# Two engines on one score group: the exponential on ScalarE and VectorE's first read of the third bank, with no order declared between them

## The chip, the cores and the metric

The kernel runs on one core of one Trainium2 chip. The metric is the device time of one execution in microseconds (us). Before the change it is 943.0 us, the median of 3 runs (941.9 to 944.33). The profile is that of one further execution, whose span is 944.2 us. The chip's engines run side by side, each through its own list of instructions in a fixed order, and they meet only through waits: TensorE multiplies matrices into PSUM, ScalarE and VectorE read PSUM and write SBUF.

## What is computed

The reference is a stack of four layers on a sequence of 2048 tokens of 448 features: softmax attention with 16 heads, then a dense block with a squared ReLU, and both once more. Each adds to `x`.

```python
def _A_ref(x, wqkv, wo):                      # attention, 16 heads of 28
    qkv = (x @ wqkv) ...                      # q, k, v: [1, 16, 2048, 28]
    scores = jnp.einsum("bhqd,bhkd->bhqk", q, k) * Dh ** -0.5
    p = _softmax(scores, axis=-1)
    o = jnp.einsum("bhqk,bhkd->bhqd", p, v)
    return o... @ wo
def _B_ref(x, w1, b1, w2, b2):                # dense, relu(h) ** 2
    h = jnp.einsum("bsd,df->bsf", x, w1) + b1
    r = jnp.where(h > 0, h, 0)
    return jnp.einsum("bsf,fd->bsd", r * r, w2) + b2

x = x + _A_ref(_layernorm(x), A_wqkv, A_wo)
x = x + _B_ref(_layernorm(x), B_w1, B_b1, B_w2, B_b2)
x = x + _A_ref(_layernorm(x), A_wqkv, A_wo)
x = x + _B_ref(_layernorm(x), B_w1, B_b1, B_w2, B_b2)
```

One layer of attention has 16 x 2048 x 2048 = 67 million scores, and each needs one exponential. The two layers of attention are where nearly all of the time lies.

## The kernel before

The scores come in **units**: one head, 256 queries, two blocks of 128 keys, which is 128 partitions x 512 columns in float32, one PSUM bank. A **group** is one tile `sc` of three banks, and there are two such tiles in turn (`ps_sc`, `bufs=2`). TensorE fills a group (line 781), ScalarE takes the exponential of it in one instruction (line 799) into `pt`, and TensorE later multiplies `pt` by the values (line 940). Two further single banks, named `mt`, serve all other products.

ScalarE would have to take all of the exponentials. So the kernel gives some units to VectorE, which computes 2^x from integer and polynomial steps. Its first operation on such a unit, the **take** (line 853), is the only one that reads the scores from PSUM; the other five work on SBUF. There are two places from which a unit is taken:

- a fourth unit of the group in one of the `mt` banks (`own` is true). ScalarE then does three banks and VectorE a bank of another tile;
- the third bank of the group's own tile (`own` is false). ScalarE then does two banks, 1024 columns, of that tile, and VectorE reads the third bank of the same tile. Only this kind is concerned by the change.

```python
def s_stream():                                  # TensorE: fills the groups
    ...
        sc = ps_sc.tile([P, 3 * 512], DT.float32, name="sc", tag="sc")
        dst = [sc[:, k * 512:k * 512 + 512] for k in range(len(us))]
        ...
            if not own:                          # the third bank goes to VectorE
                us, ks = us[:2], ks[:2]
                gbuf[gi]["n"] = 2
            us, ks = us + [units[j]], ks + [3]
            if own:
                ...                              # a bank of its own: dst.append(bank(x, "mt"))
            else:
                x = gbuf[gi]["x"] = o            # the same tile: freed by two readers
                o.need = 2
            pl.spawn(C_PRIO, a_unit(gi, x, dst[-1], us[-1], passes[us[0][0]][0]))
        ...
            nc.tensor.matmul(dst[k][...], lhsT=K_sb..., rhs=Q_sb..., start=True, stop=True, ...)   # L781

def e_stream():                                  # ScalarE: the exponentials
    ...
        pt = gbuf[gi]["pt"] = ptp.tile([P, 3 * 512], DT.bfloat16, name="pt")
        nc.scalar.activation(out=pt[:, 0:n], in_=gbuf[gi]["sc"][:, 0:n], func=AF.Exp,       # L799
                             scale=float(np.log(2.0)) * 2.0 ** -FRAC)
    o = gbuf[gi]["e"] = Op("ACT", n / 1200 + 0.05, fn, deps=[("s", gi)], acq=R_pt, need=n // 512,
                           rel=gbuf[gi]["s"], sets=("e", gi))

def a_unit(gi, x, src, unit, l):                 # VectorE: one unit
    ...
        nc.vector.tensor_scalar(out=box["i"], in0=two(src), scalar1=EXP_BIAS,               # L853
                                scalar2=EXP_LOW, op0=ALU.add, op1=ALU.max)
    c = Op("DVE", 0.69, take, deps=[("s", gi)], acq=sets_of(unit), rel=x)
    yield c
    pl.spawn(..., a_rest(...))                   # L863, L868 (three times), L874: in SBUF
```

The order of the instructions on each engine is fixed when the kernel is built: a planner (`Planner`) keeps a model of the clock of each engine, asks when an operation's `deps` have ended, and issues the earliest. In this model the exponential and the take of a group each depend on the group's matmuls, `("s", gi)`, and not on one another. The waits that end up in the program are drawn by the framework from the tiles that the instructions touch: two instructions of different engines on one tile of PSUM are put in the order in which they were issued, even when both only read.

Of the kernel before, what the change touches and what calls it, by code (L numbers as in the profile page):

```python
# [12 lines left out]
AF = mybir.ActivationFunctionType  # L13
ALU = mybir.AluOpType
# [11 lines left out]
FRAC = 16  # L26
EXP_BIAS = -0.207249953 * 2.0 ** FRAC
EXP_LOW = -56.0 * 2.0 ** FRAC
# [180 lines left out]
def kernel(  # L209
# [12 lines left out]
    nc = tc.nc  # L222
# [438 lines left out]
    gbuf = []  # L661
# [7 lines left out]
    def sets_of(unit):  # L669

        pi, kb, r, hh = unit
        l, qb, *_ = passes[pi]
        if l == 0:
            return R_v if 2 <= qb <= 6 else R_v[:1]
        return R_v
# [41 lines left out]
    def s_stream():  # L717
# [69 lines left out]
            yield o  # L787
        s_left.clear()

    def e_stream():  # L790
        gi = 0
        while gi < len(gbuf) or s_left:
            yield Op("-", 0.0, None, deps=[("s", gi)])
            n = gbuf[gi]["n"] * 512

            def fn(e, gi=gi, n=n):
                e_now[:] = [e_now[0] + n // 512 + ("x" in gbuf[gi]), gi]
                pt = gbuf[gi]["pt"] = ptp.tile([P, 3 * 512], DT.bfloat16, name="pt")
                nc.scalar.activation(out=pt[:, 0:n], in_=gbuf[gi]["sc"][:, 0:n], func=AF.Exp,  # L799
                                     scale=float(np.log(2.0)) * 2.0 ** -FRAC)  # L800
            o = gbuf[gi]["e"] = Op("ACT", n / 1200 + 0.05, fn, deps=[("s", gi)], acq=R_pt, need=n // 512,
                                   rel=gbuf[gi]["s"], sets=("e", gi))
            yield o
            gi += 1
# [25 lines left out]
    def set_of(res, l):  # L830

        k = R_v.index(res)
        two = lambda a: a.rearrange("p (a n) -> p a n", a=2)
        if k == 0:
            i, h = two(v_i[:, :]), two(v_h[:, :])
        else:
            keys = K_sb[1 - l][:, :, S - 512:S] if l == 0 else K_sb[0][:, :, 0:512]
            i, h = keys[:, 0:2, :].bitcast(DT.int32), keys[:, 2:4, :].bitcast(DT.float32)
        return i, h, two(v_e[k][:, :]), two

    def a_unit(gi, x, src, unit, l):
        yield Op("-", 0.0, None, deps=[("s", gi)])
        b0, b1, b2, b3 = [b * 2.0 ** (FRAC * (4 - k)) for k, b in enumerate(EXP_POLY)]
        box = {}

        def take(e):
            pending[0] -= 1
            box["i"], box["h"], box["e"], two = set_of(c.res, l)
            box["two"] = two
            halves = box["i"].bitcast(DT.uint16).rearrange("p a (n t) -> p a n t", t=2)  # L850
            box["f"] = halves[:, :, :, 0]
            box["n"] = box["i"].bitcast(DT.int16).rearrange("p a (n t) -> p a n t", t=2)[:, :, :, 1]
            nc.vector.tensor_scalar(out=box["i"], in0=two(src), scalar1=EXP_BIAS,  # L853
                                    scalar2=EXP_LOW, op0=ALU.add, op1=ALU.max)
        c = Op("DVE", 0.69, take, deps=[("s", gi)], acq=sets_of(unit), rel=x)
        yield c
        pl.spawn(lambda now: V_LATE if now > c.end + V_WAIT else V_PRIO, a_rest(gi, c, box, unit, (b0, b1, b2, b3)))

    def a_rest(gi, c, box, unit, bs):
        b0, b1, b2, b3 = bs  # L860

        def power(e):
            nc.vector.tensor_scalar(out=box["e"], in0=box["n"], scalar1=128.0, scalar2=128.0 * EXP_FIELD,  # L863
                                    op0=ALU.mult, op1=ALU.add)

        def step(b, begin=False):
            def fn(e):
                nc.vector.scalar_tensor_tensor(out=box["h"], in0=box["f"] if begin else box["h"], scalar=b,  # L868
                                               in1=box["f"], op0=ALU.add, op1=ALU.mult)
            return fn  # L870

        def close(e):
            pd = gbuf[gi]["pd"] = pd_of(o)
            nc.vector.scalar_tensor_tensor(out=box["two"](pd), in0=box["h"], scalar=b0,  # L874
                                           in1=box["e"].bitcast(DT.bfloat16), op0=ALU.add, op1=ALU.mult)
        h = Op("DVE", 0.68, step(b3, True), deps=[c])
        yield h
        p = Op("DVE", 0.42, power, deps=[c])
        yield p
        for b in (b2, b1):  # L880
            h = Op("DVE", 0.68, step(b), deps=[h])
            yield h
        o = Op("DVE", 0.68, close, deps=[h, p], acq=lambda: pd_free(unit), rel=c, sets=("x", gi))
        gbuf[gi]["x"] = o
        yield o
# [248 lines left out]
    pl.spawn(9.5, heat())  # L1134
    pl.spawn(0, s_stream())
    pl.spawn(1, e_stream())
    pl.spawn(2, p_stream())
    pl.clock["PE"] = 1.2
# [38 lines left out]
```

The softmax here doesn't subtract the row's maximum and nothing guards it: scores larger than these inputs give would overflow.

## Time and profile before

| | |
|---|---|
| time, median of 3 runs | 943.0 us (941.9 to 944.33) |
| span of the profiled execution | 944.2 us |
| ScalarE busy | 886.2 us (94%) |
| TensorE matmuls busy | 844.7 us (89%) |
| VectorE busy | 782.5 us (83%) |
| exponentials of three banks | 592, mean 1500 ns |
| exponentials of two banks | 76, mean 1047 ns |
| takes from `sc` | 75, some 0.69 us each |
| takes from `mt` | 45, some 0.69 us each |
| granted TensorE clock, mean | 0.989 |

A profile counts an engine as busy while an instruction of its runs. The idle time in front of an instruction is put down to whichever instruction of another engine ended last among those it waited for: "`ACT pt L799` waits for `DVE v_i L853`" says that an exponential stood idle until a take had ended. PE, DVE and ACT are TensorE, VectorE and ScalarE; names as `pt<-sc` give the tile written and the tile read. The exponentials run from 11.1 us to 924.0 us of the span, so what lies ahead of them and after them is 31 us in all.

### The profile page before, as it was taken

Reading aid. Unit: us, or ns where it says so; the run is one execution under the profiler, and the core shown is the slowest. Engines: PE = TensorE matmul, PEld = TensorE weight load, DVE = VectorE, ACT = ScalarE, POOL = GpSimd, SP = SyncE. Lnnn points to the kernel's source line nnn. Section 1 sums busy time; section 2 is a strip of 40 time slices with the busy share of each in tenths; the row PEclk is TensorE's granted clock in tenths of the full one; section 3 lists DMA queues with packets and bytes.
Section 4 is the critical chain, followed back from the end, with each engine's and each line's share of the span. In section 5 each row is a group of like instructions: output and inputs, shape, how many; then the busy total and the mean of one; then the engine's idle time right before and its main releaser. Section 6 shows DMA issues by size and latency. Waiting matters only on the chain.

```text
span 944.2 us, 29595 instructions
## 1 busy us (share of the span) xinstructions
PE 844.7 (89%) x13089; PEld 469.1 (50%) x13089; DVE 782.5 (83%) x1595; ACT 886.2 (94%) x688; POOL 42.9 (5%) x100
## 2 busy tenths in 40 slices
PE   8999888899989889998998999888988889988898
PEld 4555545354454444545444454444444545445465
DVE  7755889988999889979888888898898888888864
ACT  6999999998999999999999899999999999999993
POOL 4100000000000000010000000000000000000000
PEclk9999999999999999999999899999999999999999
DMA  7100010000000000000000000011000000000000
GB/s 233 52 2 2 9 38 14 14 13 9 13 14 9 14 14 8 14 14 2 2 2 2 1 2 1 2 43 32 23 14 18 13 23 8 24 13 19 25 9 21
DMA packets 32989, 18.47 MB, mean 20 GB/s; under 512 B 17498, under 2 KB 32411, under 8 KB 32860
## 3 DMA queue, kind: packets, MB, share of 16 engines
q1 hardware_dynamic: 32860, 16.58, 6.0%
q8 instruction: 102, 1.67, 0.7%
q14 instruction: 27, 0.22, 0.1%
HBM read 14.26 MB, written 2.07 MB: 17 GB/s over the span
## 4 chain that ended last, share of the span: by engine, by line
ACT 46%; PE 21%; DVE 18%; issue 13%; POOL 1%; DMA 1%; POOLq 0%; ACTq 0%; SPq 0%
ACT pt L799 46%; PE mt L532 9%; PE sc L781 7%; PE oT L940 3%; DVE v_h L868 2%; DVE K_sb L868 2%; DVE K_sb L853 2%; DVE v_i L853 2%; DVE r L1077 1%; DVE v_e L863 1%; DVE st L425 1%; PE mt L1128 1%; DVE xn L498 1%; DVE V_sb L874 1%; DVE x_sb L1034 1%
## 5 line engine op out<-in xcount | busy, mean ns | idle before, releaser
L799 ACT ACTIVATE pt<-sc 128x1536 bf16<-128x1536 f32 (+1 forms) x668 | 875.5, 1449 | 33.7 <-PE sc L781 15.9
L781 PE MATMUL sc<-Q_sb,K_sb 32*128 32x256 bf16 (+1 forms) x5966 | 328.1, 266 | 72.1 <-ACT pt L799 52.9
L781 PEld LDWEIGHTS <-K_sb 32*128 32x128 bf16 x6102 | 161.4, 92 | 249.9 <-issue 241.5
L940 PE MATMUL oT<-pt,V_sb 128*32 128x256 bf16 (+1 forms) x4104 | 155.5, 271 | 1.6 <-DVE K_sb L964 0.8
L532 PE MATMUL mt<-xnT,w 128*128 128x256 bf16 (+1 forms) x888 | 119.0, 272 | 6.6 <-DVE r L1077 2.7
L940 PEld LDWEIGHTS <-V_sb 128*32 128x32 bf16 x4352 | 93.8, 96 | 53.9 <-issue 50.3
L868 DVE SCALAR_TENSOR_TENSOR K_sb<-K_sb 128x512 f32<-128x512 uint16 x165 | 112.6, 683 | 0.7 <-PE mt L532 0.2
L532 PEld LDWEIGHTS <-w 128*128 128x128 bf16 x952 | 79.7, 98 | 41.4 <-issue 32.6
L868 DVE SCALAR_TENSOR_TENSOR v_h<-v_h,v_i 128x512 f32<-128x512 f32 x130 | 88.7, 683 | 0.5
L1077 DVE TENSOR_SCALAR r<-mt 128x512 bf16<-128x512 f32 x105 | 71.9, 685 | 16.1 <-PE mt L532 15.9
L532 PE MATMUL mt<-w,V_sb 128*128 128x448 bf16 (+1 forms) x288 | 68.8, 353 | 0.0
L1128 PE MATMUL mt<-xn,ident 128*128 128x448 bf16 x133 | 46.3, 359 | 3.9 <-DVE x_sb L1034 0.9
L447 POOL TENSOR_TENSOR ve<-mv,eps_t 128x2 f32<-128x2 f32 (+1 forms) x34 | 9.6, 282 | 884.1 <-DVE mv L426 814.1
L1034 DVE TENSOR_TENSOR x_sb<-x_sb,mt 128x448 bf16<-128x448 bf16 (+1 forms) x64 | 39.0, 610 | 7.1 <-PE mt L532 6.8
L868 DVE SCALAR_TENSOR_TENSOR v_h<-v_i 128x512 f32<-128x512 uint16 x65 | 44.5, 684 | 0.3
L853 DVE TENSOR_SCALAR K_sb<-sc 128x512 int32<-128x512 f32 x38 | 26.1, 688 | 18.1 <-ACT pt L799 15.1
L425 DVE BATCH_NORM_STATS2 st<-x_sb 128x6 f32<-128x448 bf16 x64 | 39.5, 617 | 1.1 <-DMA x_sb<-in_A_x_dram 0.8
L532 PEld LDWEIGHTS <-V_sb 128*128 128x128 bf16 x302 | 25.6, 98 | 24.9 <-issue 9.5
L853 DVE TENSOR_SCALAR v_i<-sc 128x512 int32<-128x512 f32 x37 | 25.4, 687 | 15.0 <-ACT pt L799 13.6
L498 DVE TENSOR_SCALAR xn<-x_sb,mv,rstd 128x448 bf16<-128x448 bf16 x64 | 25.3, 419 | 12.7 <-POOL rstd L448 12.4
L532 PE MATMUL mt<-xnT,wq 128*128 128x256 bf16 x248 | 35.2, 281 | 0.0
L532 PE MATMUL mt<-xnT,wk 128*128 128x256 bf16 x240 | 33.3, 276 | 0.1
(102 smaller groups left out, 789.8 us busy)
## 6 DMA issues: line engine op xcount, KB each, us to landing
rec<-scr SPq DMA_DIRECT2D x56, 128.0 KB
x_sb<-in_A_x_dram SPq DMA_DIRECT2D x8, 224.0 KB
out_dram<-x_sb SPq DMA_DIRECT2D x15, 112.0 KB
w<-in_B_w_dram SPq DMA_DIRECT2D x1, 1568.0 KB
w<-in_B_w_dram SPq DMA_DIRECT2D x1, 1344.0 KB
dn<-oT_sb SPq DMA_DIRECT2D x56, 4.0 KB
scr<-dn SPq DMA_DIRECT2D x56, 4.0 KB
V_sb<-in_A_wqkv_dram SPq DMA_DIRECT2D x1, 672.0 KB
```

The lines of the kernel that those rows point to most:

```text
L425: nc.vector.bn_stats(out=st[:, :], in_=x_sb[:, t0 + j, :])
L447: nc.gpsimd.tensor_tensor(out=ve[:, a:b], in0=mv[0][:, a:b, 1], in1=eps_t[:, a:b], op=ALU.add)
L498: nc.vector.tensor_scalar(out=xn[:, 0:D], in0=x_sb[:, t0 + j, :], scalar1=mv[0][:, j, 0:1], scalar2=ln[j], op0=ALU.subtract, op1=ALU.mult)
L532: nc.tensor.matmul(box["t"][:, c0:c0 + n], lhsT=lhsT() if callable(lhsT) else lhsT, rhs=rhs, start=a, stop=b)
L781: nc.tensor.matmul(dst[k][:, i * nt * P:(i + 1) * nt * P], lhsT=K_sb[l][rows, g, (kb + i) * P:(kb + i + 1) * P], rhs=Q_sb[rows, g, t0 * P: ...
L799: nc.scalar.activation(out=pt[:, 0:n], in_=gbuf[gi]["sc"][:, 0:n], func=AF.Exp, scale=float(np.log(2.0)) * 2.0 ** -FRAC)
L853: nc.vector.tensor_scalar(out=box["i"], in0=two(src), scalar1=EXP_BIAS, scalar2=EXP_LOW, op0=ALU.add, op1=ALU.max)
L868: nc.vector.scalar_tensor_tensor(out=box["h"], in0=box["f"] if begin else box["h"], scalar=b, in1=box["f"], op0=ALU.add, op1=ALU.mult)
L940: nc.tensor.matmul(box["t"][DHP * hh:DHP * hh + DHP, 0:n], lhsT=V_sb[l][:, kb + i, 4 * g + hh, :], rhs=p[:, c0:c0 + n], start=begin and kb ...
L1034: nc.vector.tensor_tensor(out=x_sb[:, tb, lo:hi], in0=x_sb[:, tb, lo:hi], in1=t[:, 0:hi - lo], op=ALU.add)
L1077: nc.vector.tensor_scalar(out=r[:, 0:w], in0=t[:, 0:w], scalar1=0.0, scalar2=None, op0=ALU.max)
L1128: nc.tensor.matmul(t[:, 0:D], lhsT=ident[:, :], rhs=xns[0][:, 0:D], start=True, stop=True)
```

## The change

For the groups whose third bank goes to VectorE, the exponential and the take are declared to need no order between them. Whichever of the two is issued second drops its wait for the first. Both still wait for the group's matmuls, and the matmuls that fill the tile anew still wait for both. No operation is added, removed, resized or moved in its engine's list. The aim is that two engines which only read, from different banks, do so at the same time.

```diff
+    def apart_from(gi, t):
+
+        if "read" in gbuf[gi]:
+            tc.declare_no_dep(t.ins, gbuf[gi]["read"].ins, reason="both read the scores, in banks of their own")
+        gbuf[gi]["read"] = t
+
     def e_stream():
 ...
-                nc.scalar.activation(out=pt[:, 0:n], in_=gbuf[gi]["sc"][:, 0:n], func=AF.Exp,
-                                     scale=float(np.log(2.0)) * 2.0 ** -FRAC)
+                t = nc.scalar.activation(out=pt[:, 0:n], in_=gbuf[gi]["sc"][:, 0:n], func=AF.Exp,
+                                         scale=float(np.log(2.0)) * 2.0 ** -FRAC)
+                if gbuf[gi].get("x") is gbuf[gi]["s"]:
+                    apart_from(gi, t)
 ...
-            nc.vector.tensor_scalar(out=box["i"], in0=two(src), scalar1=EXP_BIAS,
-                                    scalar2=EXP_LOW, op0=ALU.add, op1=ALU.max)
+            t = nc.vector.tensor_scalar(out=box["i"], in0=two(src), scalar1=EXP_BIAS,
+                                        scalar2=EXP_LOW, op0=ALU.add, op1=ALU.max)
+            if x is gbuf[gi]["s"]:
+                apart_from(gi, t)
```

## The prediction
> **What bounds the kernel now.** I read the page first (busy times, then the chain that ended last), then the groups of ScalarE's instructions with different shapes kept apart, then the waits of the exponential's line and of the take's line, and last the timeline around single groups.
>
> ```profile
> PE 844.7 (89%) x13089; PEld 469.1 (50%) x13089; DVE 782.5 (83%) x1595; ACT 886.2 (94%) x688; POOL 42.9 (5%) x100
> ACT 46%; PE 21%; DVE 18%; issue 13%; POOL 1%; DMA 1%; POOLq 0%; ACTq 0%; SPq 0%
> ```
>
> ScalarE is busiest, and the exponential's line alone is 46% of the chain. But 18% of the chain runs through VectorE and 21% through TensorE: the chain leaves ScalarE again and again. Asked by stretches, ScalarE is busy 861.6 of the 894 us between 30 and 924 us. So it idles 32 us there, and that is all that any change of waits can win in the long stretch. The groups by shape say where:
>
> ```profile
> L799 ACT ACTIVATE pt<-sc 128x1536 bf16<-128x1536 f32 x592 | 808.5, 1500 | 17.3 <-PE sc L781 15.9 <-PE oT L940 0.2
> L799 ACT ACTIVATE pt<-sc 128x1024 bf16<-128x1024 f32 x76 | 78.0, 1047 | 16.4 <-DVE K_sb L853 9.7 <-DVE v_i L853 6.3
> ```
>
> The number after the second bar is the idle time in front of the group, then who ended it. The 76 short exponentials (75 of them share their tile with a take) stand idle 16.4 us, 16.0 of it for the take on their own tile. The 592 long ones idle 17.3 us, nearly all for scores. The take's own line gives the other direction, first what it waited for, then who waited for it:
>
> ```profile
>   ACT pt L799: 28.7, 29
> ...
>   ACT pt L799: 16.0, 27
>   PE sc L781: 15.0, 25
> ```
>
> VectorE stands 28.7 us in 29 takes until the exponential of the same tile ends. And 25 times TensorE waits for a take, 15.0 us, before it can refill the tile. Both kinds stand side by side near 322 us:
>
> ```profile
> 319.75 2.42 ACT L799 ACTIVATE pt<-sc 128x1536 bf16<-128x1536 f32 x2
> 321.31 0.40 PE L781 MATMUL sc<-Q_sb,K_sb 32*128 32x256 bf16 x6
> 322.21 0.69 DVE L853 TENSOR_SCALAR K_sb<-sc 128x512 int32<-128x512 f32 x1 [0.98 <-ACT pt L799]
> 322.82 0.68 DVE L853 TENSOR_SCALAR v_i<-sc 128x512 int32<-128x512 f32 x1
> 322.95 0.40 PE L781 MATMUL sc<-Q_sb,K_sb 32*128 32x256 bf16 x6 [0.70 <-DVE K_sb L853]
> 323.59 2.37 ACT L799 ACTIVATE pt<-sc 128x1024 bf16<-128x1024 f32 x2 [1.42 <-DVE v_i L853]
> ```
>
> The exponential ends at 322.18 (its two rows are merged: 319.75 + 2.42). Only then does the take of its group start, after 0.98 us of idleness; the next group's take follows it, though that group's scores were complete at 321.71; and that group's exponential waits 1.42 us for the second take. Not one of these three waits is for data.
>
> **What the Trainium skill says.** The page "PSUM — Partial Sum Buffer", section "PSUM bank collisions raise a hardware error", says that two engines may not touch the same bank in the same 32 partitions at one time, reads against reads included, and that on different banks they ran clean. Its section "Specifications (TRN2)" quotes that ScalarE and VectorE read PSUM in parallel at full bandwidth without a collision. The trace agrees as far as it goes: 361 long exponentials overlap a VectorE instruction that reads PSUM by over 0.3 us and have a median of 1482 ns; 160 that overlap none have 1469 ns. Takes run beside an exponential of another tile already, and last 684 (from `mt`) and 690 ns (from `sc`). So reading side by side costs some 13 ns. The page "Perfetto Trace Analysis", section "Optimization Strategy", says that bubbles that repeat can mean too little PSUM for the next tile. That is the 0.70 us row above: two tiles only, and the take holds one of them.
>
> **The change part by part.** It removes one wait from each of 75 groups and leaves every engine's order as it is. In the trace the take goes first in 43 groups, the exponential in 32.
>
> *Take first (43).* The exponential's idle time sums to 16.4 us: 27 waits of 16.0 us in the view, and seven of under 0.15 us that it leaves out. Without the wait the exponential starts at the later of the previous one's end and its own scores' end. I set these side by side for all 34 in the trace. In 31 the scores were complete before the previous exponential ended, so all of the idle time goes. In three (at 218.8, 526.6 and 860.6 us) they were late by 0.34 to 0.48 us, and 1.4 us in all stays: 15.0 us. Next, the following group's scores must be there sooner. In most groups they are complete 0.35 to 0.95 us ahead of their exponential, more than is taken away; where less, the loss sums to 1.2 us: **13.8 us**.
>
> *Exponential first (32).* VectorE gets its 28.7 us back, but VectorE isn't the bound, and that by itself is worth nothing. What counts is the tile that comes free up to 0.7 us sooner:
>
> ```profile
> 711.28 0.40 PE L781 MATMUL sc<-Q_sb,K_sb 32*128 32x256 bf16 x6
> 712.18 0.69 DVE L853 TENSOR_SCALAR v_i<-sc 128x512 int32<-128x512 f32 x1 [1.38 <-ACT pt L799]
> 712.92 0.83 PE L781 MATMUL sc<-Q_sb,K_sb 32*128 32x256 bf16 x18 [0.69 <-DVE v_i L853]
> 713.86 1.45 ACT L799 ACTIVATE pt<-sc 128x1536 bf16<-128x1536 f32 x1 [0.37 <-PE sc L781]
> ```
>
> The take ends late, the refill starts late, and two groups on the exponential idles 0.37 us. This same figure, 0.36 to 0.37, comes back nine times. All idle time of the first and the second exponential after such a group sums to 5.8 us (1.2 and 4.6). I count four fifths: **4.6 us**.
>
> *All other idle time of the exponentials*, 33.7 - 16.4 - 5.8 = 11.5 us, 1.3 of it in the first 20 us. Part of it follows from late takes by way of VectorE's other work: at 531.25 us an exponential idles 1.35 us at the end of such a chain (that one is in the 4.6 above). I count a fifth of 10: **2.0 us**.
>
> *Against it.* ScalarE arrives sooner at the places where TensorE or VectorE is late for reasons of its own, and idles there instead. I take off 15% of 13.8 + 4.6: **2.8 us**. Reading side by side costs 75 x 13 ns = 1.0 us at most. The sum is 13.8 + 4.6 + 2.0 - 2.8 - 1.0 = **16.6 us**, so 943.0 - 16.6 = 926.4; I say 926.
>
> **The rivals.**
>
> *TensorE takes over as the bound.* With 89% busy it looks close, and each short exponential lets the next be due only 0.92 us later. For it: the repeats of the matmuls in line 774 fill TensorE's planned gaps. Against it: in the groups where the exponential already goes first, the one after it idles only 1.2 us in 32 cases, 0.04 us each, so TensorE holds that pace already; and the plan that set those repeats knows of no order between take and exponential. Were it true, half of 18 us would stay: 934.
>
> *The wait was hidden or comes back elsewhere* (the refill waits for the take anyway). For it: a take that VectorE starts late still holds the tile. Against it: 16.0 us is idle time of the bound engine itself. In this case the first part is worth nothing, and of the others 4.6 + 2.0 us remain: 936.
>
> *The waits feed each other,* as in the 322 us rows, where one late take delays a second group. Then most of the 10 us goes too and nothing is taken off: 13.8 + 5.8 + 7 = 27, so 916.
>
> *Slower* would need reads that disturb each other far more than 13 ns, or a granted clock that falls: between 530 and 630 us it was 0.95 already. As no order changes and only waits go, I see little of it.
>
> **Range and chances.** 918 is near the third rival, 935 near the first. The limit of 2% lies at 924.1 us, 2 us below my figure, well inside my doubt about the 15% and the fifths. So 37% for faster by over 2%, 61% for within, 2% for slower.
>
> **What would show it.** In the changed kernel's groups by shape the short exponentials' idle time falls from 16.4 to under 3 us, with no take among those who ended it; VectorE's 28.7 us of waiting for the exponential is gone; TensorE's 15.0 us for the take falls below 5; the repeated 0.37 us are gone; the long exponentials idle 10 to 15 us instead of 17.3. Their means stay within 20 ns of 1500 and 1047. I am wrong if the long ones' idle time grows by what the short ones lose (first rival), if the means grow, or if the take still waits for the exponential because some other tile orders them.

## The result and the profile after

The changed kernel takes 905.6 us (median of 4 runs, 905.13 to 906.36) beside 943.66 us of the kernel before in the same session (4 runs, 941.9 to 947.53). The ratio is 0.9592, with a 95% interval of 0.9561 to 0.9623: some 38 us less, well over twice the 16.6 us that the prediction counted, and outside its range.

First the page of the changed kernel, busy times and the chain that ended last. The exponential is now on line 805, the take on line 861.

```profile
PE 833.2 (92%) x13089; PEld 464.8 (51%) x13089; DVE 779.4 (86%) x1595; ACT 876.9 (97%) x688; POOL 42.7 (5%) x100
ACT 66%; PE 14%; issue 13%; DVE 5%; DMA 1%; POOL 0%; SPq 0%; POOLq 0%; ACTq 0%
ACT pt L805 66%; PE mt L532 6%; PE sc L781 5%; PE oT L950 2%; PE mt L1138 1%; DVE K_sb L878 1%; DMA V_sb<-in_A_wqkv_dram 1%; DVE st L425 1%; DVE xn L498 1%; DVE v_h L878 1%; DVE x_sb L1044 1%; PE sc L532 0%; PE tp L471 0%; DVE K_sb L861 0%; DVE v_i L861 0%
```

The counts of instructions are as before. VectorE's share of the chain fell from 18% to 5%, ScalarE's rose from 46% to 66%. One thing should catch the eye: ScalarE does the same work in 876.9 us of busy time, 9.3 us *less* than before. Not only idle time went.

Next ScalarE's groups with the shapes kept apart; the number after the second bar is the idle time in front of them.

```profile
L805 ACT ACTIVATE pt<-sc 128x1536 bf16<-128x1536 f32 x592 | 812.9, 1612 | 2.2 <-PE sc L781 1.7 <-PE oT L950 0.2
L805 ACT ACTIVATE pt<-sc 128x1024 bf16<-128x1024 f32 x76 | 87.4, 1197 | 0.0
```

The short exponentials' 16.4 us are gone, as predicted. But the long ones' 17.3 us are gone too, down to 2.2. And the mean durations grew by 112 and 150 ns, while the whole got shorter.

The take's own line in the changed kernel, what it waited for and then who waited for it:

```profile
  PE mt L781: 12.2, 12
  PE sc L781: 2.8, 4
who waited for it (us, times):
  PEld L781: 2.7, 7
  PE sc L781: 0.3, 1
```

No take waits for an exponential and no exponential for a take. TensorE's 15.0 us of waiting for takes became 3.0, of which 2.7 stand in front of its weight loads (PEld). The pair of groups that stood near 322 us now runs at 314 us, in the timeline:

```profile
309.61 8.81 ACT L805 ACTIVATE pt<-sc 128x1536 bf16<-128x1536 f32 x7
...
313.78 0.68 DVE L861 TENSOR_SCALAR K_sb<-sc 128x512 int32<-128x512 f32 x1
...
314.39 0.69 DVE L861 TENSOR_SCALAR v_i<-sc 128x512 int32<-128x512 f32 x1
```

Seven exponentials, both short ones among them, form one row without a gap, and the two takes run beside them. In the whole trace all 75 takes overlap the exponential of their own tile, by 0.07 to 0.69 us; before, none did.

### The profile page after: what moved, and what is told of

It reads as the page before. It is cut to its first block, busy times and chain, and to the rows that moved or that the text cites. A ratio compares the mean times of both kernels' runs of the same rounds, so it can differ in the third digit from the quotient of the medians.

```text
span 903.7 us, 29597 instructions
## 1 busy us (share of the span) xinstructions
PE 833.2 (92%) x13089; PEld 464.8 (51%) x13089; DVE 779.4 (86%) x1595; ACT 876.9 (97%) x688; POOL 42.7 (5%) x100
## 4 chain that ended last, share of the span: by engine, by line
ACT 66%; PE 14%; issue 13%; DVE 5%; DMA 1%; POOL 0%; SPq 0%; POOLq 0%; ACTq 0%
ACT pt L805 66%; PE mt L532 6%; PE sc L781 5%; PE oT L950 2%; PE mt L1138 1%; DVE K_sb L878 1%; DMA V_sb<-in_A_wqkv_dram 1%; DVE st L425 1%; DVE xn L498 1%; DVE v_h L878 1%; DVE x_sb L1044 1%; PE sc L532 0%; PE tp L471 0%; DVE K_sb L861 0%; DVE v_i L861 0%
## 5 line engine op out<-in xcount | busy, mean ns | idle before, releaser
L805 ACT ACTIVATE pt<-sc 128x1536 bf16<-128x1536 f32 (+1 forms) x668 | 866.4, 1565 | 2.2 <-PE sc L781 1.7
L950 PE MATMUL oT<-pt,V_sb 128*32 128x256 bf16 (+1 forms) x4104 | 152.3, 268 | 0.6 <-DVE K_sb L974 0.2
L1091 DVE TENSOR_TENSOR V_sb<-r 128x512 bf16<-128x512 bf16 (+1 forms) x73 | 30.3, 417 | 2.3 <-ACT r L1085 1.8
L554 DVE CAST K_sb<-mt 128x512 bf16<-128x512 f32 (+1 forms) x31 | 20.8, 672 | 12.7 <-PE mt L532 12.5
```

Source lines behind the costliest of these rows:

```text
L554: nc.vector.tensor_copy(out=dst, in_=src)
L805: t = nc.scalar.activation(out=pt[:, 0:n], in_=gbuf[gi]["sc"][:, 0:n], func=AF.Exp, scale=float(np.log(2.0)) * 2.0 ** -FRAC)
L950: nc.tensor.matmul(box["t"][DHP * hh:DHP * hh + DHP, 0:n], lhsT=V_sb[l][:, kb + i, 4 * g + hh, :], rhs=p[:, c0:c0 + n], start=begin and kb ...
L1091: nc.vector.tensor_tensor(out=h[:, 0:w // n, :], in0=r, in1=r, op=ALU.mult)
```

## The experiments

Each run is compared with the kernel before, run beside it on the same chip; its median there was 942.8 us for the first four, 942.9 for the next three and 942.3 for the last, where it was 943.66 beside the changed kernel. So the times can be set beside 905.6 to about a microsecond.

**One direction alone.** Two kernels, each with half of the change: only the exponential drops its wait, or only the take does.

```diff
-    def apart_from(gi, t):
+    def apart_from(gi, t, drop):
-        if "read" in gbuf[gi]:
+        if drop and "read" in gbuf[gi]:
# first kernel: the exponential calls it with True, the take with False; second kernel: the other way round
```

> Only the exponential drops its wait (43 groups, where the take is issued first); the take still waits for the exponential in the other 32. Theory (the waits feed each other: a take held by an exponential makes VectorE late with its other work, and that makes scores and later takes late): the short exponentials' idle time goes from 16.4 us to under 1, but the long exponentials keep most of their 17.3 us (10 to 16), and the time is 918 to 925 us. Rival (the idle time of ScalarE is all due to its own waits for takes, the long exponentials' part being a consequence of those): the long ones' idle time goes too and the time is within 4 us of the changed kernel, 905 to 910.

> Only the take drops its wait (32 groups, where the exponential is issued first); the exponential still waits for the take in the other 43. Theory (waits feed each other): the long exponentials' idle time falls from 17.3 us to under 6, the short ones' from 16.4 us to 9 to 13, since some takes were late only behind a held take; VectorE's 28.7 us are gone; time 918 to 926 us. Rival (VectorE isn't the bound, its waits are worth little: the 4.6 us of the prediction and no more): 936 to 940 us.

Measured: 922.14 us (ratio 0.9781, 0.9761 to 0.9801) when the exponential alone drops its wait, 920.52 us (0.9757, 0.9737 to 0.9776) when the take alone does. Their exponentials' rows, first kernel first:

```profile
L805 ACT ACTIVATE pt<-sc 128x1536 bf16<-128x1536 f32 x592 | 812.0, 1533 | 14.9 <-PE sc L781 13.6 <-PE oT L950 0.2
L805 ACT ACTIVATE pt<-sc 128x1024 bf16<-128x1024 f32 x76 | 82.3, 1118 | 0.5 <-PE sc L781 0.4
```

```profile
L805 ACT ACTIVATE pt<-sc 128x1536 bf16<-128x1536 f32 x592 | 804.4, 1539 | 2.7 <-PE sc L781 2.4 <-PE oT L950 0.2
L805 ACT ACTIVATE pt<-sc 128x1024 bf16<-128x1024 f32 x76 | 78.8, 1059 | 8.4 <-DVE K_sb L861 4.4 <-DVE v_i L861 3.4
```

The first removes what ScalarE itself waits for and leaves the long exponentials 14.9 us. The second takes away nothing that ScalarE waits for; only VectorE is spared its waits. Yet the long ones' idle time falls to 2.7 us, and even the short ones' is halved, to 8.4 us, just under the 9 to 13 expected. So most of the idle time for scores came from takes that had been held; of the 17.3 us, 5.6 are not there in a second profile of the kernel before (see below). Both rivals fall: it isn't ScalarE's own waits alone, and VectorE's waits are worth 22 us and not 5, though VectorE isn't the bound. The two gains sum to 42.9 us where both together give 38.1: in part they are the same delay, passed on.

The two rows of before at 322 us show how. In this stretch of the second kernel, the timeline:

```profile
317.15 2.42 ACT L805 ACTIVATE pt<-sc 128x1536 bf16<-128x1536 f32 x2
318.54 0.68 DVE L861 TENSOR_SCALAR K_sb<-sc 128x512 int32<-128x512 f32 x1
319.15 0.69 DVE L861 TENSOR_SCALAR v_i<-sc 128x512 int32<-128x512 f32 x1
319.93 2.37 ACT L805 ACTIVATE pt<-sc 128x1024 bf16<-128x1024 f32 x2 [0.36 <-DVE v_i L861]
```

The first take no longer waits for the exponential of its group, so the second take comes sooner, and the exponential that waits for the second idles 0.36 us instead of 1.42.

**Every second group.**

```diff
+            pairs.append(gi)
+            if len(pairs) % 2:
                 tc.declare_no_dep(...)
```

> Every second group, in the order of issue, drops its wait (38 of 75). If each wait costs the same wherever it stands, about 0.51 us (38 us over 75), the time is half way, 922 to 927 us. If the loss is made by few chains of waits that stand close together, removing every second link should break most of them, and the time is under 918 us. If any remaining wait passes its delay on as before, over 930 us.

Measured: 924.79 us (0.9814, 0.9791 to 0.9838), 18 us of 38 for half of the waits, with 4.8 us idle in front of the short and 10.1 us in front of the long exponentials. That is what an even spread over the groups gives; the run shows no sign of a few clusters that make the loss.

**More such waits.** The changed kernel, and the same order put on the groups whose fourth unit has an `mt` bank to itself.

```diff
+    def behind(gi, t):                   # called by the exponential and by the take of such a group
+        if "third" in gbuf[gi]:
+            tc.add_manual_dep(t.ins, gbuf[gi]["third"].ins.name, DependencyInfo(Sync, DATA), ...)
+        gbuf[gi]["third"] = t
```

> The changed kernel, with the same order between exponential and take put on the 45 groups whose fourth unit lies in an mt bank, where no order was needed before. Theory: such a wait costs some 0.5 us wherever it stands, by the idle time, the chain behind it and the lost overlap of exponentials: 905.6 + 45 x 0.5 = 928 us (920 to 936). Rival (what counts is only the third bank's hold on the score tile): under 913 us.

Measured: 940.77 us (0.9981, 0.9962 to 1.0), almost all of the gain lost again, and beyond the range expected. These 45 waits cost 35 us, 0.78 each instead of 0.5.

```profile
L812 ACT ACTIVATE pt<-sc 128x1536 bf16<-128x1536 f32 x592 | 814.0, 1521 | 29.2 <-PE sc L781 19.5 <-DVE v_i L870 6.6 <-DVE K_sb L870 1.7
```

Of the 29.2 us, 8.3 are the exponentials' own waits for takes and 19.5 are waits for scores. So the rival, that the hold on the score tile is all that counts, falls: here the take holds no score tile. The theory's size was too small. A take held in such a group waits for three banks of exponential and not for two: 18 takes wait 27.2 us, 1.5 each, where the 29 of before waited 28.7, 1.0 each. And it keeps an `mt` bank from its next use: matmuls into `mt` wait 12.3 us for takes, which they don't in the changed kernel. Which of the two makes the larger cost was not tried.

**What a held take costs: VectorE or the tile.** A take that waits does two things: it stops VectorE, and it keeps the score tile from its refill. Two kernels put back something like one of the two for the 32 groups where the take is issued second.

```diff
# VectorE held, tile free
+                if second:               # the exponential issued before this take
+                    i = nc.vector.tensor_scalar(out=idle[:, :], in0=idle[:, :], scalar1=1.0, scalar2=None, op0=ALU.mult)
+                    tc.add_manual_dep(i.ins, second.ins.name, ...)
# tile held, VectorE free
+                if second:
+                    i = nc.gpsimd.memset(hold_t[:, :], 0.0)
+                    tc.add_manual_dep(i.ins, second.ins.name, ...)
+                    gbuf[gi]["hold"] = i     # the first matmul of group gi + 2 waits for it
```

> The changed kernel; after each of the 32 takes that are issued second, VectorE gets one operation more, on a tile of its own and about as long as a take, that waits for the exponential of the group. So VectorE is held as long as before the change, but the score tile comes free as early as after it. In the run where only the exponential drops its wait, these 32 waits cost 922.1 - 905.6 = 16.5 us. Theory V (it is VectorE's lateness with its other work that costs): 915 to 923 us, and the long exponentials' idle time is back at 8 to 15 us. Rival S (it is the score tile held back from its refill): 906 to 910 us, and the long ones' idle time stays under 4 us.

> The changed kernel; for the same 32 groups the refill of the score tile waits for a memset on GpSimd of some 0.5 to 0.7 us that starts at the end of the exponential. So the tile is held about as long as before the change, and VectorE is not held. Theory V: 906 to 910 us. Rival S: 915 to 923 us, with TensorE's waits for GpSimd at 10 us or more and the long exponentials' idle time at 8 to 15 us.

Measured: 916.12 us (0.972, 0.9697 to 0.9742) with VectorE held, 913.63 us (0.9691, 0.9668 to 0.9715) with the tile held. That is 10.5 and 8.0 us over the changed kernel; together 18.5, beside the 16.5 of the 32 waits themselves. Neither theory holds alone: either path, put back by itself, costs about half. How the half is made up is less sure, since neither copy is exact. The added operations on VectorE take 0.43 us each and not 0.69; they wait for the exponential 7.0 us in all, where the held takes waited 23.8 in the kernel in which the exponential alone drops its wait, and they add 13.6 us of work. What that work costs without a wait was not tried. The memsets end some 0.64 us after the exponential, a held take 0.72.

The first line is from the kernel with VectorE held, the other two from the one with the tile held: who waited for whom, with the total, the times and the longest.

```profile
DVE idle L869 <- ACT pt L805: 7.0, 16, 0.7
PE sc L781 <- POOL hold_t L872: 12.1, 24, 1.1
ACT pt L810 <- PE sc L781: 6.8, 19, 1.3
```

**The overlap alone.** Between the changed kernel and the one before, ScalarE's busy time differs by 9.3 us. In the trace, an exponential that had to wait takes 1.451 us from its predecessor's end, idle time left out; one that follows at once adds 1.343 us. For the short ones it is 1.024 and 0.916. So whoever waits pays 0.108 us beyond the idle time. To see this without any wait for another engine, each short exponential of the changed kernel was made to wait for the exponential before it:

```diff
                 if gbuf[gi].get("x") is gbuf[gi]["s"]:
                     apart_from(gi, t)
+                    tc.add_manual_dep(t.ins, before_it[0].ins.name, DependencyInfo(Sync, DATA), ...)
+                before_it[0] = t
```

> The changed kernel, with each of the 75 short exponentials made to wait for the end of the exponential before it on the same engine. Nothing is awaited from another engine. If an exponential that has to wait loses the overlap with its predecessor, 0.108 us by the traces (1.451 less 1.343 us from end to end for long ones, 1.024 less 0.916 for short ones), this costs 75 x 0.108 = 8 us and a little for the wait itself: 912 to 917 us, with next to no idle time from other engines. If the overlap is only an artefact of how starts are recorded, 905 to 907 us.

Measured: 914.99 us (0.9707, 0.9685 to 0.9729), 9.4 us more for 75 such waits.

```profile
L807 ACT ACTIVATE pt<-sc 128x1536 bf16<-128x1536 f32 x592 | 802.6, 1521 | 2.1 <-PE sc L781 1.9
L807 ACT ACTIVATE pt<-sc 128x1024 bf16<-128x1024 f32 x76 | 78.0, 1026 | 2.4
```

The short ones' mean is *down* to 1026 ns from 1197, their idle time is 2.4 us, and the kernel is slower. 75 x 0.108 = 8.1 and 2.4 of idle time make 10.5; measured 9.4. The overlap is real.

**The kernel before once more**, unchanged, for a second profile.

> The kernel before once more, for a second profile of it. If the long exponentials' 17.3 us of idle time come of the dips of the granted clock in the first profile (0.95 between 530 and 630 us), another execution, with its dips elsewhere or without, has them elsewhere or has less; if they come of the waits, they stand within 3 us of 17.3 again.

Its single time was 938.71 us. The span is 936.9 us with a granted clock of 0.998, where the first profile had 944.2 us and 0.989.

```profile
L799 ACT ACTIVATE pt<-sc 128x1536 bf16<-128x1536 f32 x592 | 807.9, 1507 | 11.7 <-PE sc L781 10.4 <-PE oT L940 0.2
L799 ACT ACTIVATE pt<-sc 128x1024 bf16<-128x1024 f32 x76 | 78.3, 1050 | 16.5 <-DVE K_sb L853 9.8 <-DVE v_i L853 6.3
```

The short ones' idle time is the same to 0.1 us. The long ones' is 11.7 instead of 17.3 us. So some 5.6 us of what the first profile showed differ from one execution to the next. The traces say where: 4.6 us are in front of seven exponentials, at 18, 224, 226, 531, 535, 537 and 608 us of the first profile, in stretches where its clock dipped to between 0.68 and 0.88 (means of 10 us). The 10 us with the deepest dip, in the first profile and then in the second, one line each: after the length come the busy us of PE, PEld, DVE, ACT and POOL, then the clock:

```profile
530.00:540.00 10.00, 10.00 (x100) 4.10 (x99) 7.36 (x15) 6.91 (x5) 0.00 (x0) 0.68 0.01 2
530.00:540.00 10.00, 10.00 (x157) 5.98 (x157) 9.61 (x20) 10.00 (x8) 1.06 (x4) 1.00 0.01 2
```

So about a quarter to a third of the long ones' idle time stands with the dips; that the dips make it is likely by this, not tried. The other 11.7 us stood almost without dips, and most of them went with the change. The clock may have a share in the 38 us too: at a clock of 0.998 the kernel before took 938.7 to 940.0 us in three executions, the changed kernel 905.7 and 906.4, which leaves some 33 us to the change at an equal clock. Why the kernel before had a lower clock in most of its executions is open.

**A retuned plan.** With all waits inside of the plan, the planner's constants could be set anew.

```diff
-V_LATE = 3.0    KEEP = 4    HOT = 0.9     MORE = 3    OVER = 0.08
+V_LATE = 2.6    KEEP = 5    HOT = 0.95    MORE = 0    OVER = 0.09
```

> The changed kernel with five of the planner's constants moved (V_LATE 2.6 for 3.0, KEEP 5 for 4, HOT 0.95 for 0.9, MORE 0 for 3, OVER 0.09 for 0.08), chosen because the planner's own order then gives VectorE 124 units instead of 120, 84 instead of 76 of them or groups' ends as short groups. ScalarE is the bound with next to no idle time, and each unit that goes to VectorE spares it about 0.43 us (1.343 less 0.916). If the engines follow the plan now that no wait is outside of it: 900 to 905 us. If waits that the plan doesn't know still count: 906 to 915.

Measured: 902.71 us (0.9589, 0.9559 to 0.962). The median is 2.9 us under the changed kernel's, but against the kernel before the two ratios are 0.9589 and 0.9592, each with an interval of 0.003 to either side: no difference is shown.

**No repeats.** The matmuls of line 774's loop that only fill TensorE's planned gaps were left out (`MORE` 0 for 3). If TensorE had become the bound this should have taken under 902 us, and 904 to 910 if ScalarE alone is. It took 911.83 us (0.9685, 0.9659 to 0.9711), outside of both, at a granted clock of 0.983, and the kernel doesn't compute the reference's result. So nothing is built on it.

**All of them in one account.** The stretch from the first exponential's start to the last one's end, the idle time in it in front of exponentials, and the number of exponentials that start after their predecessor's end, counted in each trace. The last column is 868.1 us (the changed kernel's 871.4 less its own 2.2 and 10 x 0.108) plus the idle time plus 0.108 us for each such exponential.

| kernel | stretch, us | idle, us | with a gap | account, us |
|---|---|---|---|---|
| before | 912.9 | 33.7 | 84 | 910.9 |
| before, second profile | 905.6 | 28.2 | 77 | 904.6 |
| exponential alone drops its wait | 890.9 | 15.3 | 49 | 888.7 |
| take alone drops its wait | 885.1 | 11.1 | 39 | 883.4 |
| every second group | 889.1 | 14.9 | 50 | 888.4 |
| more waits | 906.9 | 29.3 | 66 | 904.5 |
| VectorE held | 882.4 | 9.1 | 32 | 880.7 |
| tile held | 879.7 | 7.6 | 30 | 878.9 |
| waits on ScalarE itself | 881.4 | 4.5 | 83 | 881.6 |
| changed | 871.4 | 2.2 | 10 | 871.4 |

Two terms add up to every kernel's stretch to within 2.4 us. This is book-keeping: it says that the time lies in the gaps and in the overlap that each gap ends, and not why a gap is there.

## Why the prediction was wrong, point by point

The mechanism was right: which waits go, that ScalarE bounds, that no engine's order moves. Almost every term of the sum was sized too small, and one was missing.

- **Take first, 13.8 us.** Measured: the short exponentials' 16.4 us went to 0.0. The 1.4 us held back for scores that came late, and the 1.2 us for the next group's scores, were not to be held back. They were read from a trace in which those scores were late themselves because of earlier waits: with the exponential's waits alone dropped, 0.4 us of the first and 0.9 us of the second were there, and with the takes' waits dropped as well, none of either.
- **Exponential first, 4.6 us, and all other idle time, 2.0 us.** This is the step that failed most. I looked for the damage of a held take in the first two exponentials after it and counted a fifth of the rest. Measured, the long exponentials' idle time fell from 17.3 to 2.2 us, 15.1 instead of 6.6 (from the second profile of before, 9.5; most of the rest stood in the dips of the clock). "VectorE isn't the bound, and that by itself is worth nothing" was wrong: with the takes' waits alone dropped the kernel gains 22 us, and with VectorE held and the tile free, 10.5 us come back.
- **15% off for TensorE or VectorE being late for reasons of their own, 2.8 us.** Measured: none. The long ones' idle time didn't grow, it nearly vanished. Those reasons of their own were the same waits, further back.
- **Reading side by side, 1.0 us.** Measured: none. From one end to the next, a long exponential adds 1.343 us before and after, a short one 0.916 and 0.917.
- **The missing term.** "32 us is all that any change of waits can win" left out that each gap costs 0.108 us beyond itself, inside of the busy time. 84 gaps became 10, so 74 x 0.108 = 8.0 us. This was to be read: the trace of before had an exponential's median of 1469 ns where five in a row (the row at 646.35 us, 6.82 us long) make (6.82 - 1.46) / 4 = 1.34 us each. The Trainium skill says it too, on the page "ScalarE: Activation LUTs", section "What ACT_TABLE_LOAD costs": instructions that follow at once overlap by some 93 ns. What losing the overlap costs was measured here as 108 ns.

With the measured sizes the sum is 16.4 + 15.1 + 8.0 = 39.5 us, for a difference of the profiles of 944.2 - 903.7 = 40.5. From the second profile of before it is 26.0 + 67 x 0.108 = 33.2, for 936.9 - 903.7 = 33.2. The medians' 38.1 lie between.

Of the rivals, the third was nearly right, the waits that feed each other: 27 us, and with the missing 8 it would have been 35. The first, TensorE as the next bound, fell: the exponentials idle 2.2 us in all, and TensorE's share of the chain went from 21% to 14%. So did the second, a hidden wait: the exponential's waits alone are worth 20.6 us. Of the signs, these came as written: no take among what short exponentials wait for, their idle time under 3 us, VectorE's 28.7 us gone, TensorE's 15.0 down to 3.0, the repeated 0.37 us gone. The long ones' idle time was not 10 to 15 us, and the means did not stay within 20 ns.

## What to carry to other kernels

Idle time that the trace puts down to the slow arrival of data can be the far end of a wait on an engine that isn't the bound; before such gaps are counted as lasting, ask whether what came late had itself been held by the waits that go. Only where something else holds it does the gap stay. On an engine near saturation, count the gaps as well as their length: on ScalarE each cost 0.108 us more here, the overlap with the instruction before. Where a framework draws an order between two readers of one tile, and the plan doesn't know of it, the cost can't be read from the waits of the busiest engine alone: here 16.4 us of them on ScalarE were worth 20.6 us, and 28.7 us on VectorE 22.3.

## What the runs showed of the hardware that I had not expected

An instruction's duration on ScalarE says little of its cost. A short exponential lasted 1047 ns in the mean before, 1197 after and 1026 with the wait for its predecessor, and what each added to the time was 0.917 us after and 1.024 plus its gap with the wait. The longer figure stands for the faster kernel, because an instruction that need not wait is recorded as started while the one before still runs; the median of that overlap went from 138 to 285 ns for the long ones. The distance from one end to the next is the cost.

Two engines reading different banks of one PSUM tile didn't disturb each other: the takes beside their own tile's exponential last 685 ns in the median, 690 before, and the exponentials' distance stayed at 1.343 us. This agrees with what the Trainium skill quotes on the page "PSUM — Partial Sum Buffer", section "Specifications (TRN2)", that the two read PSUM in parallel at full bandwidth without a bank collision, now for banks of the same tile.
